# A fixed order for every engine through the opening stage of a fused attention and mixture kernel

## The chip, the core and the metric

The kernel runs on one core of a Trainium2 chip. The metric is the device time of one execution in microseconds. Three executions of the kernel before took 696.54, 697.15 and 697.70 us; the median is 697.15 us. The profile shown below is of the execution that took 697.70 us; its span, from the first to the last instruction, is 695.9 us.

Five engines work side by side, each on its own queue of instructions: TensorE (PE, with its weight loads as PEld), VectorE (DVE), ScalarE (ACT), GpSimd (POOL), and SyncE (SP), which here issues all transfers.

## What is computed

The reference has three stages, each fed by the one before. Chunked attention over 4 batches, 8 heads, 768 positions and head size 64:

```python
for c in range(nc):                       # chunks of 32 queries
    k_full = concat(mem_k, k[c*32-16 : c*32+40])
    v_full = concat(mem_v, v[c*32-16 : c*32+40])
    scores = scale * q_c @ k_full.T
    a = exp(scores - max(scores)); a = a / (sum(a) + 1e-9)
    out[c] = a @ v_full
```

Then a feed-forward layer over 3072 tokens, and a soft mixture of 8 experts:

```python
h = x @ w_in                              # 512 -> 2048
g = s * relu(h)**2 + b
y = g @ w_out                             # 2048 -> 512
logits = y @ phi                          # 32 slots
slot_input = softmax(logits, axis=0).T @ y
slot_out[e] = relu(slot_input[e] @ w1[e]) @ w2[e]
result = softmax(logits, axis=1) @ slot_out
```

## The kernel before, in words

The 3072 tokens are taken in six blocks of 512 (`NB`). A block has four **attention units** u, one for each pair of heads. The hidden layer has sixteen tiles of 128 (`NF`), so the feed-forward part is 96 steps n; step n takes hidden tile n mod 16 of block n div 16. A step issues 12 products into the hidden tile (`mm_h`), the activation (`make_g`), and, one step later, 12 products into the output (`mm_y`). Every operand is split into a high and a low part of a rounded format, so each product is three matmuls; ACT makes the high part and another engine subtracts it for the low part.

While PE works through block j, the attention of block j+1 and the mixture's statistics of block j-1 are slipped in between (`bg`). Only the four units of block 0 have nothing to hide behind: they run in an opening stage, before the first steps, and that stage is what the change rewrites.

The feed-forward weights come as 64-bit integers' worth of halves: 32 halves of 512 columns (two for each hidden tile: first the w_in half, then the w_out half), each loaded into a staging tile `sp`, decoded by four instructions and stored in `w`. The decode is one clamp on DVE, two passes on ACT, and a join on DVE (`w_decode`).

An attention unit goes through these instructions in turn: the query tile is spread into a block layout by ACT and DVE (`spread_q`); 16 small matmuls give the scores (`att_qk`, with a DVE memset or two on the scores' bank for the edges of the sequence); DVE takes the maximum and subtracts it, ACT takes the exponential, DVE sums, adds a constant and takes the reciprocal, and POOL multiplies (`att_soft`); PE transposes four blocks and two copies bring them to `pb` (`att_tr`); 16 small matmuls multiply with the values (`att_pv`), ACT writes the high part of x and DVE the low part.

The opening stage is written as a string of tokens, `START`, a letter and a number each. Letters: q, k, v and w are loads, c loads constants, z is a warming matmul on zeros, S spreads q, A is the score matmuls, F the softmax, T and t the transposes with their copies (T with both copies on ACT), P the value matmuls with both parts of x, D a decode, I and O the splits of the w_in and w_out half, H the first step's products with one of the four x tiles, y frees buffers.

Before the change, only PE and SP keep the order in which the code is written. For ACT, DVE and POOL a scheduler chooses the order, over the opening stage and the steps behind it together.

```python
    with tc.manual_schedule(engines={mybir.EngineType.PE, mybir.EngineType.SP}):
...
        for token in START.split():
            steps[token[0]](int(token[1:]))
```

Whatever is chosen, each engine then works through its list strictly in order, and an instruction that waits holds up everything behind it on that engine.

Of the kernel before, what the change touches and what calls it, by code (L numbers as in the profile page):

```python
# [11 lines left out]
AF = mybir.ActivationFunctionType  # L12
ALU = mybir.AluOpType
# [23 lines left out]
def tile_attention_moe_softmoe(  # L37
# [83 lines left out]
    def r32(ap):  # L121
        return ap.bitcast(F32R)
# [41 lines left out]
    def spread_q(u):  # L164
        t, src = qv(u), qsv(u)
        act.activation(out=t[0:64, :, 0, :], in_=src[0:64], func=AF.Copy)
        dve.tensor_copy(t[64:128, :, 1, :], src[64:128])

    def load_v(u):
        j, hp = divmod(u, NHP)  # L170
# [17 lines left out]
            if gc % 24 == 23:  # L188
                dve.memset(S[64 * par:64 * par + 64, t, 56:64], NEG)

    def att_soft(u, b, last=None):
        S = b.rearrange("p (t n) -> p t n", t=8)
        E = epv(u)
        mx, sm = ast[u % 2][:, 0, :], ast[u % 2][:, 1, :]
        dve.tensor_reduce(out=mx, in_=S, axis=AX.X, op=ALU.max)  # L195
        dve.tensor_tensor(out=E, in0=S, in1=mx.unsqueeze(2).to_broadcast([P, 8, 64]), op=ALU.subtract)  # L196
        act.activation(out=E, in_=E, func=AF.Exp, scale=0.125)  # L197
        dve.tensor_reduce(out=sm, in_=E, axis=AX.X, op=ALU.add)  # L198
        dve.tensor_scalar(out=sm, in0=sm, scalar1=EPS, scalar2=None, op0=ALU.add)  # L199
# [16 lines left out]
    def att_pv(u, b):  # L216
        j, hp = divmod(u, NHP)
        vt, pb = vv(u), pbv(u)
        for m in range(8):
            for h in range(2):  # L220
                pe.matmul(b[64 * h:64 * h + 64, 64 * m:64 * m + 64], lhsT=vt[:, m, h, :],  # L221
                          rhs=pb[:, m // 2, m % 2, h].rearrange("p z n -> p (z n)"), start=True, stop=True)
        xt = hl(X[j % 2][hp])
        act.activation(out=r32(xt[:, 0]), in_=b, func=AF.Copy)  # L224
        dve.tensor_tensor(out=r32(xt[:, 1]), in0=b, in1=xt[:, 0], op=ALU.subtract)  # L225


# [11 lines left out]
            sp.dma_start(out=t.bitcast(U32), in_=wd[f][:, 512 * h:512 * h + 512].bitcast(U32))  # L239
            stage_full.append((f, h, t))  # L240

    def w_decode():
        f, h, t = stage_full.pop(0)
        u = t.bitcast(U32).rearrange("p (n w) -> p n w", w=2)
        low, high = u[:, :, 0], u[:, :, 1]
        hv = t.rearrange("p (n w) -> p n w", w=2)[:, :, 1]
        top = t.bitcast(U8).rearrange("p (n b) -> p n b", b=8)[:, :, 3]
        dst = W[f][:, 512 * h:512 * h + 512].bitcast(U32)
        dve.tensor_scalar(out=hv, in0=hv, scalar1=-EXP_TOP, scalar2=EXP_TOP, op0=ALU.max, op1=ALU.min)
        act.activation(out=hv, in_=hv, func=AF.Prelu, scale=EXP_SHIFT, alpha=SIGN_SHIFT)  # L250
        act.activation(out=low, in_=top, func=AF.Copy, scale=1.0 / 32.0, bias=-31.0 / 64.0)
        dve.scalar_tensor_tensor(out=dst, in0=high, scalar=3, in1=low, op0=ALU.logical_shift_left,
                                 op1=ALU.bitwise_or)
        stage_free.append(t)


    def split_wi(n):
        t, raw = hl(WI[n % 2]), W[n % NF][:, 0:512]
        act.activation(out=r32(t[:, 0]), in_=raw, func=AF.Copy)  # L259
        (dve if n < NF else pool).tensor_tensor(out=r32(t[:, 1]), in0=raw, in1=t[:, 0], op=ALU.subtract)  # L260

    def split_wo(n):
        t, raw = hl(WO[n % 2]), W[n % NF][:, 512:1024]
# [197 lines left out]
    def run_bg(task):  # L461
        k, a = task
        if k == "qk":
            b = mbank()
            att_qk(a, b)
            if a + 2 < NB * NHP:
                load_q(a + 2)
                load_k(a + 2)
            att_soft(a, b)
        elif k == "tr":  # L470
            att_tr(a, mbank())
        elif k == "pv":
            att_pv(a, mbank())
            if a + 2 < NB * NHP:
                load_v(a + 2)
        elif k == "log":
            y_logits(a, mbank())
        elif k == "ytr":
            y_tr(a, mbank(), "act" if a % 2 else "dve")
        elif k == "etr":  # L480
            b = mbank()
            pe.transpose(b[:, 128:256], lts, ident)
            e_tr(b)
            dve.tensor_copy(lall[:, 4 * a:4 * a + 4, :], b[:, 128:256].rearrange("p (t s) -> p t s", t=4))
        elif k == "csoft":
            c_soft(a)
        elif k == "slot":
            slots(a, mbank())

    with tc.manual_schedule(engines={mybir.EngineType.PE, mybir.EngineType.SP}):  # L490
# [26 lines left out]
        def s_qk(u):  # L517
            sbk[u] = sbank()
            att_qk(u, sbk[u])


        steps = {
            "c": lambda _: sp.dma_start(out=cons, in_=cd),
# [3 lines left out]
            "S": spread_q,  # L527
            "w": w_load,
            "z": keep_warm,
            "t": lambda u: att_tr(u, sbank()),  # L530
            "A": s_qk,
            "F": lambda u: att_soft(u, sbk[u], pool),
            "T": lambda u: att_tr(u, sbank(), True),
            "P": lambda u: att_pv(u, sbank()),
            "D": lambda _: w_decode(),
            "I": split_wi,
            "O": split_wo,
# [279 lines left out]
```

## Time and profile before

| | us |
|---|---|
| median of 3 executions | 697.15 (696.54 to 697.70) |
| profiled execution | 697.70 |
| its span, first to last instruction | 695.9 |
| PE busy | 675.7 (97% of the span) |
| DVE busy | 357.7 (51%) |
| ACT busy | 353.6 (51%) |
| POOL busy | 216.7 (31%) |
| TensorE's mean granted clock | 0.99 of full |

PE is busy nearly throughout, so its gaps decide; they are few and lie at the two ends. A busy PE is not PE at its peak, since the ends of matmuls are modelled. The other engines are half busy on average, but that average hides one stretch, from 35 to 110 us, where DVE is nearly full.

### The profile page before, as it was taken

To read this page: it belongs to the slowest core of one execution; us is meant where nothing else is said; L and a number is where in the kernel's file an instruction comes from. 1 tells how busy PE (TensorE), PEld (TensorE's weight loads), DVE (VectorE), ACT (ScalarE), POOL (GpSimd) and SP (SyncE) were. 2 spreads that over 40 slices of the span, in tenths; PEclk is the share of its full clock that TensorE was granted. 3 is DMA by queue.
4 is the path that set the end of the run, shared out by engine and by line. 5 is a ranking of instruction groups with operands and counts; after the bars stand their busy time and mean duration, and the time that the engine had idled before them with its cause. 6 is when DMAs were issued, how large, how long until landed. Compare 5 with 4: busy or idle time off the path is not lost.

```text
span 695.9 us, 12228 instructions
## 1 busy us (share of the span) xinstructions
PE 675.7 (97%) x4953; PEld 533.3 (77%) x4953; DVE 357.7 (51%) x644; ACT 353.6 (51%) x628; POOL 216.7 (31%) x178
## 2 busy tenths in 40 slices
PE   7599999999999999999999999999999999999995
PEld 4488888888788888788888788888788888787353
DVE  5689997446534456544445444554553332223233
ACT  4779894544444445444445444545444544444332
POOL 4100000343344334334434334434334444441000
PEclk9799999999999999999999999999999999999998
DMA  9998802702201211211120221120123523628998
GB/s 348 389 336 328 270 40 91 284 32 80 91 16 77 91 42 50 91 52 64 68 75 18 91 67 56 61 91 1 62 84 129 211 92 91 211 92 272 237 294 348
DMA packets 47032, 94.38 MB, mean 136 GB/s; under 512 B 2944, under 2 KB 27520, under 8 KB 46976
## 3 DMA queue, kind: packets, MB, share of 16 engines
q1 hardware_dynamic: 46976, 93.60, 39.3%
q8 instruction: 39, 0.64, 0.4%
q14 instruction: 17, 0.14, 0.1%
HBM read 87.30 MB, written 6.29 MB: 134 GB/s over the span
## 4 chain that ended last, share of the span: by engine, by line
PE 95%; DVE 2%; ACT 1%; POOL 1%; issue 0%; POOLq 0%; DVEq 0%; ACTq 0%
PE bank L292 39%; PE bank L272 38%; PE bank L221 4%; PE bank L181 3%; PE bank L686 2%; PE bank L643 2%; PE bank L207 2%; PE bank L336 1%; PE bank L712 1%; PE bank L314 1%; PE bank L352 1%; PE bank L504 1%; PE bank L390 0%; POOL rt L201 0%; PE bank L662 0%
## 5 line engine op out<-in xcount | busy, mean ns | idle before, releaser
L292 PE MATMUL bank<-g,wo 128*128 128x512 f32 x1152 | 285.2, 396 | 0.0
L272 PE MATMUL bank<-x,wi 128*128 128x512 f32 x1152 | 278.6, 391 | 0.0
L272 PEld LDWEIGHTS bank<-x,wi 128*128 128x128 f32 x1152 | 217.1, 189 | 45.2
L292 PEld LDWEIGHTS bank<-g,wo 128*128 128x128 f32 x1152 | 211.1, 188 | 48.9 <-ACT wi L259 4.2
L279 DVE SCALAR_TENSOR_TENSOR rt<-bank,cons,rt 128x512 f32<-128x512 f32 x96 | 72.0, 750 | 228.3 <-ACT rt L278 228.1
L265 POOL TENSOR_TENSOR wo<-w,wo 128x512 fp32r<-128x512 f32 x80 | 103.2, 1290 | 204.9 <-ACT wo L264 200.9
L260 POOL TENSOR_TENSOR wi<-w,wi 128x512 fp32r<-128x512 f32 x80 | 103.4, 1293 | 188.8 <-ACT wi L259 188.8
L259 ACT ACTIVATE wi<-w 128x512 fp32r<-128x512 f32 x96 | 60.5, 630 | 148.3 <-PE bank L272 144.8
L280 ACT ACTIVATE g<-rt,cons 128x512 fp32r<-128x512 f32 x96 | 69.4, 723 | 42.6 <-DVE rt L279 41.3
L264 ACT ACTIVATE wo<-w 128x512 fp32r<-128x512 f32 x96 | 60.3, 628 | 55.2 <-PE bank L292 53.5
L281 DVE SCALAR_TENSOR_TENSOR g<-rt,cons,g 128x512 fp32r<-128x512 f32 x96 | 72.0, 750 | 27.3 <-ACT g L280 24.5
L278 ACT ACTIVATE rt<-bank 128x512 f32<-128x512 f32 x96 | 55.8, 581 | 5.4 <-PE bank L272 5.2
L197 ACT ACTIVATE ep<-ep 128x512 f32<-128x512 f32 x22 | 13.8, 627 | 30.1 <-DVE ep L196 30.1
L221 PEld LDWEIGHTS bank<-pb,v 128*64 128x64 f32 x704 | 22.3, 138 | 7.1 <-issue 6.7
L181 PEld LDWEIGHTS bank<-k,q 128*64 128x64 f32 x704 | 22.4, 138 | 5.6 <-issue 4.5
L181 PE MATMUL bank<-k,q 128*64 128x64 f32 x704 | 24.7, 223 | 1.7 <-ACT ep L197 1.7
L221 PE MATMUL bank<-pb,v 128*64 128x64 f32 x704 | 25.3, 225 | 0.0
L198 DVE TENSOR_REDUCE ast<-ep 128x8 f32<-128x512 f32 x22 | 15.1, 685 | 9.8 <-ACT ep L197 9.7
L225 DVE TENSOR_TENSOR x<-bank,x 128x512 fp32r<-128x512 f32 x24 | 16.5, 688 | 0.6 <-ACT x L224 0.5
L224 ACT ACTIVATE x<-bank 128x512 fp32r<-128x512 f32 x24 | 14.3, 596 | 4.9 <-PE bank L221 2.5
L195 DVE TENSOR_REDUCE ast<-bank 128x8 f32<-128x512 f32 x24 | 16.4, 683 | 0.4
L199 DVE TENSOR_SCALAR ast<-ast 128x8 f32<-128x8 f32 x24 | 15.9, 664 | 0.7
(237 smaller groups left out, 522.6 us busy)
## 6 DMA issues: line engine op xcount, KB each, us to landing
k<-kd SPq DMA_DIRECT2D x22, 512.0 KB, 6.1
sp<-wd SPq DMA_DIRECT2D x22, 512.0 KB, 8.8
v<-vd SPq DMA_DIRECT2D x22, 512.0 KB, 3.9
q<-qd SPq DMA_DIRECT2D x20, 512.0 KB, 5.3
w<-e1d SPq DMA_DIRECT2D x10, 512.0 KB, 3.4
out<-w SPq DMA_DIRECT2D x9, 512.0 KB, 6.2
sp<-e1d SPq DMA_DIRECT2D x7, 512.0 KB, 7.9
sp<-e2d SPq DMA_DIRECT2D x7, 512.0 KB, 7.2
```

Of the source, the lines that this page charges most:

```text
L181: pe.matmul(S[64 * par:64 * par + 64, 2 * i + z, :], lhsT=qt[:, c].rearrange("p h n -> p (h n)"), rhs=kt[:, c, :], start=True, stop=True)
L221: pe.matmul(b[64 * h:64 * h + 64, 64 * m:64 * m + 64], lhsT=vt[:, m, h, :], rhs=pb[:, m // 2, m % 2, h].rearrange("p z n -> p (z n)"), sta ...
L259: act.activation(out=r32(t[:, 0]), in_=raw, func=AF.Copy)
L260: (dve if n < NF else pool).tensor_tensor(out=r32(t[:, 1]), in0=raw, in1=t[:, 0], op=ALU.subtract)
L264: act.activation(out=r32(t[:, 0]), in_=raw, func=AF.Copy)
L265: (dve if n < NF else pool).tensor_tensor(out=r32(t[:, 1]), in0=raw, in1=t[:, 0], op=ALU.subtract)
L272: pe.matmul(HB[n % 2], lhsT=r32(w[:, a, kt, :]), rhs=r32(x[:, b]), start=(kt == 0 and i == 0), stop=(kt == 3 and i == 2))
L278: act.activation(out=r, in_=HB[n % 2], func=AF.Relu, scale=1.0 / WSCALE ** 2)
L279: dve.scalar_tensor_tensor(out=t, in0=HB[n % 2], scalar=s_col, in1=r, op0=ALU.mult, op1=ALU.mult)
L280: act.activation(out=r32(g[:, 0]), in_=t, func=AF.Identity, bias=b_col)
L281: dve.scalar_tensor_tensor(out=r32(g[:, 1]), in0=t, scalar=b_col, in1=g[:, 0], op0=ALU.add, op1=ALU.subtract)
L292: pe.matmul(YB[dt], lhsT=r32(w[:, a, dt * 128:dt * 128 + 128]), rhs=r32(g[:, b]), start=(f == 0 and i == 0), stop=(f == NF - 1 and i == 2))
```

## The change

The string is rewritten and its steps are cut finer. The softmax is split into m (maximum, subtraction, exponential) and n (sum, reciprocal, multiplication on POOL); the value matmuls P no longer include the low part of x, which is x; a decode is D (clamp and the two ACT passes) and E (the join); the split of a w_in half is I and i. The DVE half of spreading q moves to POOL for every unit but the first. T3 gets one of its two copies on DVE, and T0 both on ACT. One warming matmul is added ahead of A0, and two instead of one stand between A0 and A1. The loads of the second and third staged halves come later in the list of transfers. And the whole string is put under a fixed order for ACT, DVE and POOL too.

```diff
 START = (
-    "q0 k0 w1 c0 q1 k1 q2 k2 v0 w1 q3 k3 v1 w1 v2 v3 w1 "
-    "z3 S0 A0 F0 z1 S1 D0 A1 z1 S2 t0 z1 A2 P0 F1 S3 T1 F2 "
-    "I0 A3 k4 w1 q4 w1 k5 P1 v4 w1 T2 q5 H0 P2 F3 T3 P3 y0 H1 w9 H2 D0 v5 D0 D0"
+    "q0 k0 w1 c0 q1 k1 q2 k2 v0 q3 k3 v1 w1 v2 w1 v3 w1 "
+    "z4 S0 A0 z1 D0 m0 S1 z1 A1 E0 n0 S2 I0 m1 A2 T0 i0 n1 m2 z1 S3 P0 T1 A3 x0 n2 m3 D1 P1 x1 T2 E1 n3 H0 D2 P2 x2 E2 "
+    "k4 w1 q4 w1 k5 v4 w1 q5 H1 T3 P3 H2 x3 D3 E3 y0 w9 v5"
 )
...
         act.activation(out=t[0:64, :, 0, :], in_=src[0:64], func=AF.Copy)
-        dve.tensor_copy(t[64:128, :, 1, :], src[64:128])
+        (pool if u else dve).tensor_copy(t[64:128, :, 1, :], src[64:128])
...
-    def att_soft(u, b, last=None):
+    def att_exp(u, b):
         S = b.rearrange("p (t n) -> p t n", t=8)
-        E = epv(u)
-        mx, sm = ast[u % 2][:, 0, :], ast[u % 2][:, 1, :]
+        E, mx = epv(u), ast[u % 2][:, 0, :]
...
+    def att_norm(u, last=None):
+        E, sm = epv(u), ast[u % 2][:, 1, :]
...
+    def att_low(u, b):
+        j, hp = divmod(u, NHP)
+        xt = hl(X[j % 2][hp])
         dve.tensor_tensor(out=r32(xt[:, 1]), in0=b, in1=xt[:, 0], op=ALU.subtract)
...
+    def w_end():
+        f, h, t = half_done.pop(0)
+        low, high, hv, top, dst = w_views(f, h, t)
         dve.scalar_tensor_tensor(out=dst, in0=high, scalar=3, in1=low, op0=ALU.logical_shift_left,
                                  op1=ALU.bitwise_or)
...
-        for token in START.split():
-            steps[token[0]](int(token[1:]))
+        with tc.manual_schedule(engines={mybir.EngineType.Activation, mybir.EngineType.DVE, mybir.EngineType.Pool}):
+            for token in START.split():
+                steps[token[0]](int(token[1:]))
```

What this does to the lists of the engines is seen in three places. First, ACT's list at its beginning. `q0` and `q1` are the spread queries of units 0 and 1, `sp0` the first staged half, `ep` the exponentials, `w14` holds the raw queries of units 2 and 3. Before:

```order
L166 ACTIVATE q0_97<-rt1_96 64x16x32
L251 ACTIVATE sp0_110<-sp0_110 128x512
L250 ACTIVATE sp0_110<-sp0_110 128x512
L166 ACTIVATE q1_98<-rt1_96 64x16x32
L259 ACTIVATE wi0_81<-w0_65 128x512
L197 ACTIVATE ep_109<-ep_109 128x512
L166 ACTIVATE q0_97<-w14_79 64x16x32
```

The same place in the changed kernel:

```order
L166 ACTIVATE q0_97<-rt1_96 64x16x32
L262 ACTIVATE sp0_110<-sp0_110 128x512
L263 ACTIVATE sp0_110<-sp0_110 128x512
L196 ACTIVATE ep_109<-ep_109 128x512
L166 ACTIVATE q1_98<-rt1_96 64x16x32
L166 ACTIVATE q0_97<-w14_79 64x16x32
L280 ACTIVATE wi0_81<-w0_65 128x512
```

The spread of q1 has moved behind the exponential of unit 0 (L196, L197 before), and the order of the decode's two passes is swapped.

Second, DVE's list at its beginning. `bank1` and `bank2` hold the scores of units 0 and 1, `ast0` and `ast1` their maxima and sums. Before:

```order
L167 COPY q0_97<-rt1_96 64x16x32
L249 TENSOR_SCALAR sp0_110<-sp0_110 128x512
L187 MEMSET bank1_140 64x16
L195 TENSOR_REDUCE ast0_135<-bank1_140 128x8
L252 SCALAR_TENSOR_TENSOR w0_65<-sp0_110 128x512
L196 TENSOR_TENSOR ep_109<-bank1_140,ast0_135 128x512
L167 COPY q1_98<-rt1_96 64x16x32
L260 TENSOR_TENSOR wi0_81<-w0_65,wi0_81 128x512
L198 TENSOR_REDUCE ast0_135<-ep_109 128x8
L167 COPY q0_97<-w14_79 64x16x32
L199 TENSOR_SCALAR ast0_135<-ast0_135 128x8
L187 MEMSET bank2_141 64x16
```

The same place in the changed kernel:

```order
L167 COPY q0_97<-rt1_96 64x16x32
L187 MEMSET bank1_140 64x16
L261 TENSOR_SCALAR sp0_110<-sp0_110 128x512
L194 TENSOR_REDUCE ast0_135<-bank1_140 128x8
L195 TENSOR_TENSOR ep_109<-bank1_140,ast0_135 128x512
L187 MEMSET bank2_141 64x16
L269 SCALAR_TENSOR_TENSOR w0_65<-sp0_110 128x512
L200 TENSOR_REDUCE ast0_135<-ep_109 128x8
L201 TENSOR_SCALAR ast0_135<-ast0_135 128x8
L202 RECIPROCAL ast0_135<-ast0_135 128x8
L194 TENSOR_REDUCE ast1_136<-bank2_141 128x8
L195 TENSOR_TENSOR ep_109<-bank2_141,ast1_136 128x512
```

The memset on each unit's scores, which waits for that unit's score matmuls, now stands ahead of the clamp of sp0 (for unit 0) and ahead of the join of w0 and of unit 0's sum (for unit 1).

Third, DVE's list from unit 3's maximum (the reduce on `bank1`) to its reciprocal (on `ast1`); `x01` and `x02` are the x tiles of units 1 and 2, `rt0` holds the exponentials of units 2 and 3. Before:

```order
L195 TENSOR_REDUCE ast1_136<-bank1_140 128x8
L265 TENSOR_TENSOR wo0_83<-w0_65,wo0_83 128x512
L225 TENSOR_TENSOR x01_86<-bank2_141,x01_86 128x512
L196 TENSOR_TENSOR rt0_95<-bank1_140,ast1_136 128x512
L249 TENSOR_SCALAR sp2_112<-sp2_112 128x512
L198 TENSOR_REDUCE ast1_136<-rt0_95 128x8
L252 SCALAR_TENSOR_TENSOR w1_66<-sp2_112 128x512
L225 TENSOR_TENSOR x02_87<-bank6_145,x02_87 128x512
L199 TENSOR_SCALAR ast1_136<-ast1_136 128x8
L260 TENSOR_TENSOR wi1_82<-w1_66,wi1_82 128x512
L200 RECIPROCAL ast1_136<-ast1_136 128x8
```

The same place in the changed kernel:

```order
L194 TENSOR_REDUCE ast1_136<-bank1_140 128x8
L195 TENSOR_TENSOR rt0_95<-bank1_140,ast1_136 128x512
L261 TENSOR_SCALAR sp1_111<-sp1_111 128x512
L261 TENSOR_SCALAR sp4_114<-sp4_114 128x512
L231 TENSOR_TENSOR x01_86<-bank2_141,x01_86 128x512
L269 SCALAR_TENSOR_TENSOR w0_65<-sp1_111 128x512
L200 TENSOR_REDUCE ast1_136<-rt0_95 128x8
L201 TENSOR_SCALAR ast1_136<-ast1_136 128x8
L293 TENSOR_TENSOR wo0_83<-w0_65,wo0_83 128x512
L202 RECIPROCAL ast1_136<-ast1_136 128x8
```

The low part of x01 and the split of wo0 (L293) now stand between unit 3's subtraction and its reciprocal, and so does work of later steps, which the scheduler has put between the fixed instructions: the clamp of `sp4` is not in the string. ACT's list has the same in that place: between the two copies of T2 and those of T3 stand, in this order, a pass of sp4, the high part of wo0, the other pass of sp4, one of sp5, two of sp2 and the high part of x02.

## Rows read from the trace of the kernel before

**Rows 1.** The page: PE's busy share in 40 equal slices of the span.

```profile
PE   7599999999999999999999999999999999999995
```

**Rows 2.** Busy us (instructions) of PE, PEld, DVE, ACT, POOL by stretch; clock, DMA share, GB/s.

```profile
0.00:35.00 35.00, 23.17 (x288) 15.40 (x289) 21.93 (x47) 20.39 (x34) 9.17 (x17) 0.88 0.94 367
35.00:110.00 75.00, 75.00 (x521) 61.68 (x521) 71.22 (x138) 62.92 (x112) 0.00 (x0) 0.99 0.69 245
110.00:600.00 490.00, 490.00 (x3272) 399.21 (x3271) 234.54 (x400) 234.95 (x413) 193.33 (x150) 1.00 0.23 79
```

**Rows 3.** PE's waits up to 42 us: total us, times, longest.

```profile
PE bank L207 <- POOL rt L201: 5.8, 2, 3.4
```

**Rows 4.** Timeline of PE: start us, us, what, [idle before <-releaser].

```profile
1.31 5.08 PE L504 MATMUL bank<-w 128*128 128x512 f32 x6 [1.31 <-POOL w L500]
6.32 1.15 PE L181 MATMUL bank<-k,q 128*64 128x64 f32 x32
7.40 1.12 PE L504 MATMUL bank<-w 128*128 128x512 f32 x2
10.26 1.15 PE L181 MATMUL bank<-k,q 128*64 128x64 f32 x32 [1.74 <-ACT ep L197]
...
13.49 0.66 PE L207 MATMUL bank<-cons,ep 128*128 128x128 f32 x4 [1.02 <-POOL ep L201]
...
14.94 1.15 PE L181 MATMUL bank<-y,q 128*64 128x64 f32 x32
...
18.23 1.15 PE L181 MATMUL bank<-y,q 128*64 128x64 f32 x32 [0.28 <-ACT q L166]
...
22.88 1.11 PE L207 MATMUL bank<-cons,rt 128*128 128x128 f32 x4 [2.40 <-POOL rt L201]
...
25.34 1.59 PE L221 MATMUL bank<-pb,yt 128*64 128x64 f32 x32
30.32 1.12 PE L207 MATMUL bank<-cons,rt 128*128 128x128 f32 x4 [3.40 <-POOL rt L201]
32.80 1.97 PE L221 MATMUL bank<-pb,yt 128*64 128x64 f32 x32 [1.36 <-ACT pb L212]
34.70 5.91 PE L272 MATMUL bank<-x,wi 128*128 128x512 f32 x21
...
41.62 3.02 PE L292 MATMUL bank<-g,wo 128*128 128x512 f32 x12
```

**Rows 5.** Timeline of POOL, ACT and DVE: one of each kind of instruction.

```profile
3.47 0.52 POOL L512 MEMSET pb<- 64x512 f32 x1
6.89 0.67 ACT L250 ACTIVATE sp<-sp 128x512 f32<-128x512 f32 x1
8.27 0.68 DVE L252 SCALAR_TENSOR_TENSOR w<-sp 128x512 uint32<-128x512 uint32 x1
9.59 0.63 ACT L197 ACTIVATE ep<-ep 128x512 f32<-128x512 f32 x1
10.65 0.68 DVE L198 TENSOR_REDUCE ast<-ep 128x8 f32<-128x512 f32 x1
11.36 0.42 DVE L167 COPY q<-w 64x512 f32<-64x512 f32 x1
12.02 0.20 DVE L200 RECIPROCAL ast<-ast 128x8 f32<-128x8 f32 x1
12.40 1.04 POOL L201 TENSOR_TENSOR ep<-ep,ast 128x512 f32<-128x512 f32 x1 [6.54 <-DVE ast L200]
35.45 0.69 DVE L225 TENSOR_TENSOR x<-bank,x 128x512 fp32r<-128x512 f32 x1 [0.20 <-ACT x L224]
```

**Rows 6.** PE by stretch: busy us (instructions), granted clock, DMA share, GB/s.

```profile
20.00:23.00 3.00, 0.60 (x19) 0.99 1.03 419
23.00:26.00 3.00, 2.94 (x19) 0.50 1.02 415
30.00:36.00 6.00, 4.32 (x39) 0.50 0.76 294
```

More of the change, by code (lines that the diff above doesn't have):

```diff
@@ L240, in w_load, with w_views @@
             stage_full.append((f, h, t))
-    def w_decode():
-        f, h, t = stage_full.pop(0)
+    def w_views(f, h, t):
         u = t.bitcast(U32).rearrange("p (n w) -> p n w", w=2)
@@ L248, in w_decode, with w_begin @@
         dst = W[f][:, 512 * h:512 * h + 512].bitcast(U32)
+        return low, high, hv, top, dst
+    half_done = []
+    def w_begin():
+        f, h, t = stage_full.pop(0)
+        low, high, hv, top, dst = w_views(f, h, t)
         dve.tensor_scalar(out=hv, in0=hv, scalar1=-EXP_TOP, scalar2=EXP_TOP, op0=ALU.max, op1=ALU.min)
@@ L251, in w_decode @@
         act.activation(out=low, in_=top, func=AF.Copy, scale=1.0 / 32.0, bias=-31.0 / 64.0)
+        half_done.append((f, h, t))
+    def w_end():
+        f, h, t = half_done.pop(0)
+        low, high, hv, top, dst = w_views(f, h, t)
         dve.scalar_tensor_tensor(out=dst, in0=high, scalar=3, in1=low, op0=ALU.logical_shift_left,
@@ L254, in w_decode, with wi_high, wi_low, split_wi @@
         stage_free.append(t)
-    def split_wi(n):
+    def w_decode():
+        w_begin()
+        w_end()
+    def wi_high(n):
         t, raw = hl(WI[n % 2]), W[n % NF][:, 0:512]
         act.activation(out=r32(t[:, 0]), in_=raw, func=AF.Copy)
+    def wi_low(n):
+        t, raw = hl(WI[n % 2]), W[n % NF][:, 0:512]
         (dve if n < NF else pool).tensor_tensor(out=r32(t[:, 1]), in0=raw, in1=t[:, 0], op=ALU.subtract)
+    def split_wi(n):
+        wi_high(n)
+        wi_low(n)
     def split_wo(n):
@@ L468, in run_bg @@
                 load_k(a + 2)
-            att_soft(a, b)
+            att_exp(a, b)
+            att_norm(a)
         elif k == "tr":
@@ L472, in run_bg @@
         elif k == "pv":
-            att_pv(a, mbank())
+            b = mbank()
+            att_pv(a, b)
+            att_low(a, b)
             if a + 2 < NB * NHP:
@@ L519, in s_qk, with s_pv @@
             att_qk(u, sbk[u])
+        def s_pv(u):
+            sbk[u] = sbank()
+            att_pv(u, sbk[u])
         steps = {
@@ L529, in tile_attention_moe_softmoe @@
             "z": keep_warm,
-            "t": lambda u: att_tr(u, sbank()),
             "A": s_qk,
[L532 to L537, printed above, removed]
+            "m": lambda u: att_exp(u, sbk[u]),
+            "n": lambda u: att_norm(u, pool),
+            "T": lambda u: att_tr(u, sbank(), u < 3),
+            "P": s_pv,
+            "x": lambda u: att_low(u, sbk[u]),
+            "D": lambda _: w_begin(),
+            "E": lambda _: w_end(),
+            "I": wi_high,
+            "i": wi_low,
             "H": lambda kt: mm_h(0, (kt,)),
```

## The prediction

> **What bounds the kernel now.** I began with the page's slices: PE stands at nine tenths or more from the third slice on, and only the first two and the last show room [rows 1]. The busy times by stretch make that exact. From 35 to 110 us PE is busy 75.00 of 75.00 us, from 110 to 600 us 490.00 of 490.00, but only 23.17 of 35 us in the opening stage [rows 2]. So from 35 us PE sets the pace and has no gap in which lost time could be won back, and whatever moves the start of the first output products (L292 in the timeline, 41.62 us, [rows 4]) moves the end by the same amount. I call that start Y0; the forecast is how far it moves.
>
> In the opening stage nothing is full: DVE is busy 21.93 of 35 us and ACT 20.39 [rows 2]. It is a chain. The waits of PE say which: 5.8 us for POOL's multiplication in units 2 and 3, the longest 3.4 us [rows 3], that is the end of a softmax that crosses PE, DVE, ACT, DVE and POOL. The timeline gives the steps: A0 at 6.32, A1 10.26, T0 13.49, A2 14.94, A3 18.23, T2 22.88, P2 25.34, T3 30.32, P3 32.80, then 21 feed-forward matmuls from 34.70 to 40.6, and Y0 [rows 4].
>
> **The change part by part.** Almost nothing is added or removed: one warming matmul, three copies moved from DVE to POOL. What changes is what stands ahead of what on each engine, so I walked the new lists from A0 to Y0, each instruction starting when its engine and its inputs are ready, with the durations of the timeline: sum, join, subtraction and low part 0.69 on DVE, reciprocal 0.20 and the constant before it 0.17, decode pass 0.67 and exponential 0.63 on ACT, multiplication 1.04 on POOL [rows 5], score matmuls 1.15 [rows 4]. The same walk over the old lists puts T3 at 30.3 and Y0 at 41.6, where the trace has 30.32 and 41.62, so the method is worth about half a us.
>
> The one operation without a row is POOL's copy of 64x512. Below it stands POOL's memset of the same shape, 0.52; above it a copy with twice the data and a second input would be the multiplication, 1.04; DVE does the copy in 0.42 [rows 5]. With a margin I use 0.5 to 1.2 as ends and 0.85 as value, between the two POOL rows. The Trainium skill (GPSIMD Engine Reference, Engine selection) says that a one-input operation runs on GpSimd at about the rate of VectorE, which no run here shows yet; by it each copy would cost about 0.42 and, with two copies on the chain, my sum would come out 0.9 us smaller.
>
> *A0.* The first three warming matmuls take 5.08 us, 0.85 for each of six records; the later ones take 1.12 for two records [rows 4]. The fourth costs about 1.0 at that rate. A0 moves from 6.32 to 7.4: **+1.1**.
>
> *A1.* The score matmuls end at 8.55. DVE's list now has the memset on them first, so the clamp of sp0, which ran while A0 was still running, comes after: memset 0.07, clamp 0.42, maximum 0.69, subtraction 0.69, to 10.5. ACT follows with the exponential to 11.15, and only then with its half of q1's spread, which now stands behind it: 11.75. A1 starts at 11.8 instead of 10.26: **+1.5**. The old list had this spread done early; A1 did not depend on unit 0's softmax.
>
> *A2 and T0.* A1 ends at 12.95. The memset on unit 1's scores now stands ahead of the join of w0 and of unit 0's sum, so a softmax whose exponential was ready at 11.15 waits for A1. Then 0.07, 0.69, 0.69, 0.17, 0.20 and small gaps: reciprocal at 14.9, POOL's multiplication to 16.0. POOL's list is in order too: its copy for q2 stands behind it, to 16.9. A2 waits for that: 16.9 instead of 14.94, **+2.0**. T0, ready at 16.0, stands behind A2 in PE's list: 17.9 at full clock, against 13.49.
>
> Here the clock enters. In the old run PE idled 2.4 us ahead of T2, and the stretch from 23 to 26 us shows 0.50 granted, the lower of the two levels; the same again from 30 to 36 us, after the idle 3.4 us [rows 4, 6]. Between A1 and A2 PE will now idle about 4 us, longer than either. So I take A2 and T0 at the lower level, as T2 and P3 were (1.11 and 1.97 instead of 0.66 and 1.15, [rows 4]): T0 at 18.9, **+5.4** (+4.4 at full clock).
>
> *A3 and T2.* The same pattern twice more. The memset on unit 2's scores holds wi0's low part and unit 1's sum; then multiplication, copy for q3, and ACT's half of the spread behind unit 2's exponential: A3 at 23.8 instead of 18.23, **+5.6** (+4.5). The memset on unit 3's scores holds x00's low part and unit 2's sum: reciprocal at 26.9, T2 at 28.0 instead of 22.88, **+5.1** (+4.0).
>
> *P2 and T3.* ACT now has unit 3's exponential, two passes of sp1 and the high part of x01 ahead of T2's copies: from 28.3, 0.63 + 2 x 0.67 + 0.60 + 2 x 0.59, so P2 starts at 31.9 instead of 25.34. Behind the copies stand a pass of sp4 and the high part of wo0, to 33.1; DVE's reciprocal for unit 3 stands behind wo0's low part: 33.8, then 34.0, POOL to 35.1. T3 at 35.1 instead of 30.32, **+4.8** (+3.7).
>
> *P3 to Y0.* ACT has two passes of sp2 and x02 ahead of T3's first copy, DVE the low part of x02 and a join ahead of the second: P3 at 38.1 instead of 32.80. At the lower clock it ends at 40.1; high and low part of x03 are there at 41.7, against 36.14 in the old run [rows 5]: **+5.5**. H1 has been done by then, which gives back some tenths. Fifteen matmuls and the score matmuls of unit 4 take PE to 46.5. On ACT, the high part for step 2, two passes of sp3, the activation, a pass of sp0 and wo1's high part stand ahead of the first g: 46.9. Y0 at about 46.6 instead of 41.62: **+5.0**.
>
> *Costed at nothing.* The three copies taken from DVE (3 x 0.42) give nothing, since DVE is waiting where they stood. The later loads of sp1 and sp2 cost nothing, since their decodes start at 28 us, long after; the same holds for the transfers behind them on SP's queue that now wait for sp2 and sp3 to be joined, as they bring weights of step 4 and later, 20 us ahead of use. If that cover were gone PE would stall in the steps (third rival). From Y0 on the lists hold the same work, and at Y0 one staged half more has been joined than before.
>
> The profiled execution took 697.7; with +5.0 it is 702.7. The median of the runs shown lies 0.55 below that execution, so I forecast **702.2**. Full clock throughout and a copy of 0.5 give +3.2 (then the first g, behind ACT's list, is what Y0 waits for); a copy of 1.2 and the lower clock up to Y0 give +6.5.
>
> **The rivals.** *Faster: the idle time fills.* DVE idles 13 and ACT 15 of the first 35 us [rows 2]; three units in flight could fill this, remove the waits of 5.8 us before T2 and T3 [rows 3], and, less the 1.1 for the warming matmul and about as much for the clock, give -3.5: 693.7. The Trainium skill speaks for it (Perfetto Trace Analysis, Optimization Strategy): interleaving regimes with different limits may improve performance. What decides is whether T3 starts before 30.3. Against it, T3 depends on A3's softmax, A3 on POOL's copy behind unit 1's multiplication, and that on A2: in the list the units are chained to each other more than before. Chance 0.08.
>
> *No change.* If POOL's copies cost little and the memsets rarely held DVE, A2 and A3 would keep their old times, T3 would start within 1.4 us of 30.3, and the end would stay within 0.2% (1.4 us, about what this kernel's measurement can tell from nothing): 697.2. Against it, the first +1.5 at A1 rests only on rows of PE, DVE and ACT that are known. Chance 0.06.
>
> *Slower by more: PE starves in the decode stretch.* DVE is busy 71.22 of 75 us from 35 to 110 us [rows 2]. If its order there is worse, or halves arrive late because SP waits for sp3's join (about 45 us), PE would wait before some of the first 14 steps, for a few tenths to a us each: 3 to 6 us more, about 706.5. It decides if any weight split ends after PE has finished the step before. Against it, DVE starts the stretch one half ahead. Chance 0.12.
>
> **How the numbers follow.** My own case has 0.74, at 702.2, with 700.4 to 703.7 as its bounds. To leave out no more than 2 in 10 the range takes in half of the slower rival's span, up to 705.5, and reaches down to 699.0 for a walk that errs by more than its test showed; the faster case and no change stay out (0.14). Faster 0.08, same 0.06, slower 0.86.
>
> **What the profile after would show.** A1 near 11.8, A2 near 16.9 with its wait put down to POOL's copy of q, T0 behind A2, T3 near 35, Y0 near 46.6, and PE busy without a gap from there, each later step shifted alike. I am wrong if A2 starts by 15.5, if T3 starts before 31, or if PE's steps after Y0 are closer or wider apart than before. The copy on POOL should take 0.5 to 1.2; the granted clock should be at its lower level at A2 or T0.

## The result and the profile after

The changed kernel takes **702.76 us** (median; 701.87 to 703.67), the kernel before 697.42 (696.54 to 698.53): a ratio of 1.0076 with an interval of 1.0056 to 1.0096, slower by 5.3 us. The profiled execution took 703.02, its span is 701.2.

First the timeline of PE in the changed kernel, start and duration in us, with the idle time ahead and what ended it:

```profile
1.31 6.14 PE L535 MATMUL bank<-w 128*128 128x512 f32 x8 [1.31 <-POOL w L531]
7.38 1.15 PE L181 MATMUL bank<-k,q 128*64 128x64 f32 x32
...
11.75 1.15 PE L181 MATMUL bank<-k,q 128*64 128x64 f32 x32 [1.31 <-ACT q L166]
16.62 1.98 PE L181 MATMUL bank<-y,q 128*64 128x64 f32 x32 [3.72 <-ACT ep L196]
18.53 1.12 PE L209 MATMUL bank<-cons,ep 128*128 128x128 f32 x4
...
22.95 1.15 PE L181 MATMUL bank<-y,q 128*64 128x64 f32 x32 [0.27 <-issue]
...
27.13 0.66 PE L209 MATMUL bank<-cons,rt 128*128 128x128 f32 x4 [1.37 <-POOL rt L203]
...
30.67 1.98 PE L223 MATMUL bank<-pb,yt 128*64 128x64 f32 x32 [2.19 <-ACT pb L214]
...
34.02 1.05 PE L209 MATMUL bank<-cons,rt 128*128 128x128 f32 x4
37.00 1.97 PE L223 MATMUL bank<-pb,yt 128*64 128x64 f32 x32 [1.92 <-DVE pb L216]
38.90 5.05 PE L300 MATMUL bank<-x,wi 128*128 128x512 f32 x18
43.88 1.15 PE L181 MATMUL bank<-k,q 128*64 128x64 f32 x32
44.99 3.01 PE L320 MATMUL bank<-g,wo 128*128 128x512 f32 x12
...
57.58 0.66 PE L209 MATMUL bank<-cons,ep 128*128 128x128 f32 x4 [1.41 <-DVE ep L203]
...
59.24 3.03 PE L320 MATMUL bank<-g,wo 128*128 128x512 f32 x12
```

The rows are to be laid beside [rows 4]. A0 is 1.06 later, A1 1.49, A2 1.68, T0 5.04, A3 4.72, T2 4.25, P2 5.33, T3 3.70, P3 4.20 and Y0 (44.99) 3.37. The second thing to see is the row at 57.58: PE, dense from Y0 on in the kernel before, waits 1.41 us ahead of unit 4's transposes, between the output products of steps 1 and 2. I call the start of step 2's output products Y2. It goes from 54.25 to 59.24, 4.99 later, and every later step I looked at lies 5.0 later (128.24 and 133.25, 551.31 and 556.32). So the opening costs 3.4, of which 1.06 is there at A0, behind the fourth warming matmul, and 2.31 arises from A0 to Y0. This wait and what goes with it cost 1.6. The last 0.3 is idle time of PE at the far end (8.6 us behind 600 us, 8.3 before).

The stretches of the changed kernel, PE, PEld, DVE, ACT and POOL busy, clock, DMA share, GB/s:

```profile
0.00:35.00 35.00, 24.08 (x260) 15.90 (x260) 16.63 (x39) 17.65 (x29) 11.07 (x20) 0.88 0.94 365
35.00:110.00 75.00, 71.67 (x529) 58.86 (x529) 70.44 (x135) 63.58 (x114) 0.00 (x0) 0.96 0.62 227
110.00:600.00 490.00, 490.00 (x3272) 399.18 (x3271) 238.05 (x407) 235.18 (x413) 191.44 (x148) 1.00 0.23 81
...
16.00:20.00 4.00, 3.38 (x37) 3.04 (x38) 1.30 (x4) 0.94 (x2) 0.57 (x1) 0.57 1.03 410
20.00:24.00 4.00, 3.49 (x70) 2.48 (x68) 1.59 (x4) 3.12 (x7) 1.65 (x2) 1.00 1.03 409
30.00:40.00 10.00, 7.41 (x74) 6.08 (x75) 8.47 (x16) 8.05 (x14) 1.05 (x1) 0.51 0.64 251
40.00:44.00 4.00, 4.00 (x21) 3.01 (x21) 3.49 (x7) 3.16 (x7) 0.00 (x0) 0.95 0.00 0
```

Beside [rows 2] DVE does 5.3 us less work in the first 35 us and ACT 2.7 less: 1.3 of DVE's are the copies now on POOL; for the rest the fixed lists leave both idle, and the work comes after. From 35 to 110 us PE lacks 3.33 us, the wait of 1.92 ahead of P3 and that of 1.41 in step 2. In the last row the DMA engines move nothing for 4 us.

How a fixed list loses time is best seen on DVE at unit 0's softmax, start, duration and idle time:

```profile
9.78 0.69 DVE L195 TENSOR_TENSOR ep<-bank,ast 128x512 f32<-128x512 f32 x1
12.96 0.67 DVE L269 SCALAR_TENSOR_TENSOR w<-sp 128x512 uint32<-128x512 uint32 x1 [2.49 <-ACT q L166]
12.98 0.07 DVE L187 MEMSET bank<- 64x16 f32 x1
13.55 0.68 DVE L200 TENSOR_REDUCE ast<-ep 128x8 f32<-128x512 f32 x1
...
14.47 0.20 DVE L202 RECIPROCAL ast<-ast 128x8 f32<-128x8 f32 x1
```

and on POOL behind it:

```profile
14.85 1.04 POOL L203 TENSOR_TENSOR ep<-ep,ast 128x512 f32<-128x512 f32 x1 [4.78 <-DVE ast L202]
15.96 0.61 POOL L167 COPY q<-w 64x512 f32<-64x512 f32 x1
```

Unit 0's exponential has ended at 11.13. Its sum (L200) starts at 13.55, behind the memset on unit 1's scores, which A1 makes (11.75 to 12.90), while DVE is idle for 2.49 us. The profile names ACT's spread (L166) for this wait, but both spreads have ended by 12.2; what ends last ahead of it is A1. POOL's multiplication waits for the reciprocal, the copy for q2 behind it, and A2 for that copy, which ends at 16.57. The profile puts A2's wait down to unit 1's exponential, which ends at 16.62 but feeds nothing of A2; in e3 below, where the two again end within 0.1 of each other, it names POOL's copy.

The wait in step 2 is found in two views. SP's longest wait from 34 to 70 us, by total, times, longest:

```profile
SPq L245 <- DVE w L269: 15.8, 5, 6.8
```

and the chain of work that ended last, from 43.96 on (start, us, what):

```profile
43.96 0.37 SPq L245
...
44.43 7.30 DMA yt<-wd
...
51.74 0.02 ACT yt L263
51.77 0.54 issue
52.31 0.59 ACT rt L306
...
56.92 0.61 DVE ep L203
...
57.58 0.66 PE bank L209 x4
```

SP stands 6.8 us at a transfer that needs a staging tile back from a join; the transfers into `yt` and `y` stand behind it, though their tiles are free by 39 (P3, which reads yt last, ends at 38.97). They go out at 43.95, after the 4 us in which nothing moved. ACT's list has the decode passes on yt ahead of step 2's activation (L306), so ACT waits until 51.74, then DVE's list runs late, down to the multiplication that unit 4's transposes need.

### The profile page after: what moved, and what is told of

Its sections match the earlier page's. It is cut to its first block, busy times and chain, and to the rows that moved or that the text cites. A ratio compares the mean times of both kernels' runs of the same rounds, so it can differ in the third digit from the quotient of the medians.

```text
span 701.2 us, 12236 instructions
## 1 busy us (share of the span) xinstructions
PE 678.3 (97%) x4955; PEld 535.1 (76%) x4955; DVE 355.8 (51%) x641; ACT 353.5 (50%) x628; POOL 219.0 (31%) x181
## 4 chain that ended last, share of the span: by engine, by line
PE 92%; DMA 3%; DVE 2%; ACT 1%; issue 1%; POOL 0%; SPq 0%; ACTq 0%; POOLq 0%
PE bank L320 38%; PE bank L300 36%; PE bank L223 4%; PE bank L181 3%; PE bank L681 2%; PE bank L724 2%; PE bank L209 1%; PE bank L364 1%; DMA v<-vd 1%; DMA yt<-wd 1%; PE bank L342 1%; PE bank L535 1%; PE bank L380 1%; PE bank L750 1%; DMA out<-w 1%
## 5 line engine op out<-in xcount | busy, mean ns | idle before, releaser
L293 POOL TENSOR_TENSOR wo<-w,wo 128x512 fp32r<-128x512 f32 x80 | 103.3, 1292 | 205.3 <-ACT wo L292 205.3
L306 ACT ACTIVATE rt<-bank 128x512 f32<-128x512 f32 x96 | 55.7, 581 | 4.6 <-PE bank L300 4.6
L196 ACT ACTIVATE ep<-ep 128x512 f32<-128x512 f32 x22 | 13.8, 627 | 28.4 <-DVE ep L195 28.2
L200 DVE TENSOR_REDUCE ast<-ep 128x8 f32<-128x512 f32 x22 | 15.1, 685 | 9.1 <-ACT ep L196 9.0
L262 ACT ACTIVATE sp<-sp 128x512 f32<-128x512 f32 x24 | 15.9, 671 | 7.5 <-DVE sp L261 7.4
L269 DVE SCALAR_TENSOR_TENSOR w<-sp 128x512 uint32<-128x512 uint32 x24 | 17.0, 718 | 3.5 <-ACT q L166 2.5
```

The lines of the kernel that those rows point to most:

```text
L306: act.activation(out=r, in_=HB[n % 2], func=AF.Relu, scale=1.0 / WSCALE ** 2)
```

## The experiments

All times are medians, ratios are to the kernel before on the same chip, whose median there was 697.81, 697.86 or 698.28. A0 itself lies anywhere from 5.6 to 8.0 in the profiled executions, by how many warming matmuls there are and how long they take, so I compare the way from A0 to Y0. The starts are from PE's timelines (us), each of one profiled execution, which can lie off its kernel's median (e9: 693.86 beside 695.44; e3: 702.37 beside 701.13):

| kernel | A0 | T0 to P0 | T3 | Y0 | A0 to Y0 | Y0 to Y2 | time |
|---|---|---|---|---|---|---|---|
| before | 6.32 | 2.43 | 30.32 | 41.62 | 35.30 | 12.63 | 697.4 |
| changed | 7.38 | 2.41 | 34.02 | 44.99 | 37.61 | 14.25 | 702.8 |
| e1 order not fixed | 7.66 | 4.64 | 31.03 | 41.85 | 34.19 | 12.63 | 698.1 |
| e2 copies on DVE | 7.62 | 2.52 | 32.20 | 44.27 | 36.65 | 12.87 | 700.2 |
| e3 q1 first | 7.98 | 2.76 | 33.41 | 45.23 | 37.25 | 13.87 | 701.1 |
| e4 loads as before | 7.09 | 2.41 | 33.73 | 44.60 | 37.51 | 12.81 | 701.4 |
| e5 units first | 7.30 | 2.41 | 30.58 | 44.63 | 37.33 | 13.25 | 703.1 |
| e6 before, fixed | 6.53 | 3.31 | 40.47 | 59.02 | 52.49 | 12.64 | 715.0 |
| e7 fixed, reordered | 7.56 | 1.95 | 28.54 | 45.05 | 37.49 | 12.63 | 700.1 |
| e8 free, three edits | 6.37 | 2.42 | 26.97 | 37.73 | 31.36 | 12.82 | 693.5 |
| e9 free, copies on DVE | 6.75 | 2.50 | 26.87 | 37.33 | 30.58 | 12.63 | 695.4 |
| e10 free, three warming | 5.64 | 5.56 | 30.79 | 42.10 | 36.46 | 12.63 | 698.2 |
| e11 free, loads as before | 6.82 | 5.63 | 31.17 | 41.68 | 34.86 | 12.62 | 698.0 |

My theory was that the fixed order is the loss, because ready work stands behind waiting work; the rivals were that the new list, the copies on POOL or the fourth warming matmul are. The fourth warming matmul is taken out alone only with the order free (e10), not with the order fixed.

**The new list without the fixed order** (e1).

```diff
-        with tc.manual_schedule(engines={mybir.EngineType.Activation, mybir.EngineType.DVE, mybir.EngineType.Pool}):
-            for token in START.split():
-                steps[token[0]](int(token[1:]))
+        for token in START.split():
+            steps[token[0]](int(token[1:]))
```

> The changed kernel with the fixed order of ACT, DVE and POOL taken away; the new string, the finer steps, POOL's copies and the order of the transfers stay. Theory (the loss is in what stands ahead of what on the three engines): Y0, the start of the first output products, falls from 44.99 to between 38 and 41.6 us, and the time to between 695 and 698.5, at or below the kernel before. Rival (the loss is in the string itself: the extra warming matmul, the copies on POOL, the later loads): Y0 stays above 43.5 and the time above 701.

698.09 us, ratio 1.000 (0.999 to 1.0011). The whole loss is gone, the wait in step 2 too. Y0 at 41.85 is just past the late end of the range: PE waits in a new place, at P0.

```profile
16.06 0.66 PE L209 MATMUL bank<-cons,ep 128*128 128x128 f32 x4 [1.70 <-POOL ep L203]
...
20.70 1.98 PE L223 MATMUL bank<-pb,v 128*64 128x64 f32 x32 [3.12 <-ACT pb L214]
```

ACT in the same kernel:

```profile
18.86 0.69 ACT L263 ACTIVATE sp<-sp 128x512 uint32<-128x512 uint8 x1 [1.43 <-DMA sp<-wd]
19.45 0.57 ACT L212 ACTIVATE pb<-bank 64x512 f32<-64x512 f32 x1
20.05 0.59 ACT L214 ACTIVATE pb<-bank 64x512 f32<-64x512 f32 x1
```

T0's copies (L212, L214) stand behind a decode pass on a half that lands at 18.8. A free order has its own such mistakes; this one comes back below.

**The kernel before with a fixed order** (e6), the other half of this test: on the lists as its own string writes them.

```diff
-        for token in START.split():
-            steps[token[0]](int(token[1:]))
+        with tc.manual_schedule(engines={mybir.EngineType.Activation, mybir.EngineType.DVE, mybir.EngineType.Pool}):
+            for token in START.split():
+                steps[token[0]](int(token[1:]))
```

> The kernel before with one edit: ACT, DVE and POOL keep the order in which its own opening list is written, as the changed kernel does with its list. Theory: the fixed order is itself the cost, since as written the pieces of a softmax stand ahead of ready work of other units; the order that the scheduler finds for the kernel before is much better than its list. Walking the fixed lists with the durations of before, T3 starts at about 37 instead of 30.3 and Y0 at 50 to 56 instead of 41.6, so the time is 706 to 712. Rival: what costs is the new list (pieces, copies on POOL), not fixing as such. Then this kernel stays within 1 us of 697.4.

714.97 us, ratio 1.0245 (1.0228 to 1.0262): the theory's side, and 3 us more than its range. PE's waits show where:

```profile
24.96 1.12 PE L207 MATMUL bank<-cons,ep 128*128 128x128 f32 x4 [5.93 <-POOL ep L201]
...
40.47 1.11 PE L207 MATMUL bank<-cons,rt 128*128 128x128 f32 x4 [6.60 <-POOL rt L201]
```

So fixing alone costs some 17 us, the new list alone nothing, both together 5.3. The new list wins back most of what fixing takes away, but not all; which of its parts does so (finer pieces, their order, the copies) no run takes apart.

**The three copies back on DVE, order fixed** (e2).

```diff
-        (pool if u else dve).tensor_copy(t[64:128, :, 1, :], src[64:128])
+        dve.tensor_copy(t[64:128, :, 1, :], src[64:128])
```

> The changed kernel with the DVE half of every spread of q back on DVE; all else stays, the fixed order too. Theory (A2 and A3 start late since POOL's copy stands behind a multiplication): the copies for units 2 and 3 no longer wait for a softmax, A2 comes some 2 us earlier, Y0 near 42 and the time near 699.5 to 700.5. Rival (A2 and A3 wait for the softmax by other ways, PE's and DVE's lists): Y0 stays within 0.7 of 44.99 and the time within 1 of 702.8.

700.24 us, ratio 1.0029 (1.0015 to 1.0044). The time is as expected, the way there is not: A0 to Y0 is only 0.96 shorter, and Y0 to Y2 1.38, since PE has no wait in step 2 left. In that run yt's transfer goes out 1.63 ahead of Y0 instead of 1.04, and ACT no longer waits for it.

**q1's spread ahead of unit 0's softmax** (e3).

```diff
-    "z4 S0 A0 z1 D0 m0 S1 z1 A1 ...
+    "z4 S0 A0 z1 S1 D0 m0 z1 A1 ...
```

> The changed kernel with one token moved: the spread of q1 (S1) stands ahead of the decode and of unit 0's maximum, subtraction and exponential. Theory (ACT's half of it waits for the exponential, and with A1 everything behind it): A1 starts near 10.3 instead of 11.75, Y0 near 42.5 to 43.5, the time near 700.5. Rival (the chain is held elsewhere, so an earlier A1 only lengthens the waits): A1 moves, Y0 stays within 0.5 of 44.99 and the time within 1 of 702.8.

701.13 us, ratio 1.0044 (1.0028 to 1.0059). A1 comes 1.38 earlier behind A0, Y0 only 0.36: for Y0 the rival was right, and the time lies between the two. A2 then waits 3.7 us for POOL's copy of q. One place mended, the chain waits at the next.

**The late loads in the order of before** (e4): the tiles yt and y are put second in the list of free staging tiles instead of last.

```diff
-            "y": lambda _: stage_free.extend(YT + Y),
+            "y": lambda _: stage_free.__setitem__(slice(1, 1), YT + Y),
```

> The changed kernel with the list of late loads in the order of before: behind the eighth staged half come the yt and y buffers, and the buffers sp1 to sp3, which wait for their joins, come last. Theory (SP waits for sp3's join until 43.95, the transfers pause, ACT then waits for yt until 51.7 and PE 1.4 us in step 2): Y0 stays at 45, the 1.4 us ahead of the transposes of unit 4 go to under 0.4, and the time is near 701.3. Rival (that wait comes from DVE's list, not from the transfers): the 1.4 us and 702.8 stay.

701.4 us, ratio 1.0049 (1.0031 to 1.0067). A0 to Y0 is unchanged (37.51 beside 37.61), Y0 to Y2 takes 12.81 instead of 14.25, and the row of 1.41 is gone: 1.44 us, as the theory had it. This rests on the trace; the time fits it (701.4 beside 702.76), but its interval overlaps that of the change. In place of the empty 4 us the same stretches now read:

```profile
40.00:42.00 2.00, 2.00 (x10) 1.59 (x9) 2.00 (x5) 1.36 (x3) 0.00 (x0) 1.00 0.97 324
42.00:44.00 2.00, 2.00 (x23) 1.45 (x24) 1.58 (x3) 2.00 (x5) 0.00 (x0) 1.00 0.95 246
```

**Units 2 and 3 ahead of the decodes, order fixed** (e5). Beside e1 the changed kernel is 1.0 us later at T2, 3.0 at T3 and 3.2 at P3, so it loses 2.2 us between T2 and P3 (the 3.0 below is the lag at T3). I took this stretch for the place.

```diff
-    "... A3 x0 n2 m3 D1 P1 x1 T2 E1 n3 H0 D2 P2 x2 E2 "
-    "k4 w1 q4 w1 k5 v4 w1 q5 H1 T3 P3 H2 x3 D3 E3 y0 w9 v5"
+    "... A3 x0 n2 m3 P1 T2 n3 x1 H0 P2 D1 T3 x2 E1 P3 x3 "
+    "k4 w1 q4 w1 k5 v4 w1 q5 H1 H2 D2 E2 D3 E3 y0 w9 v5"
```

> The changed kernel with its fixed list rewritten behind unit 3's exponential: the tokens of unit 2's and 3's transposes and products (P1 T2 n3 x1 H0 P2 T3 x2 P3 x3) go ahead of the decode passes of sp1, sp2 and sp3 (D1 E1, D2 E2, D3 E3), so that neither two passes of sp1 nor x01 stand ahead of T2's copies and only one decode stands between T2 and T3's copies. Against the kernel with the free order, the changed kernel loses 3.0 us between T2 and P3 and 3.1 at Y0. Theory: these last links of the attention chain are what sets Y0. Then T3 starts at about 31 instead of 34.0, P3 at about 34 instead of 37.0, Y0 at about 42 instead of 45.0, and the time is 699.8 (699 to 700.6). Rival: Y0 is set as much by the decodes that feed steps 0 to 2, which this edit puts 1 to 3 us later on ACT and DVE. Then T3 and P3 come early all the same, but PE waits for the parts of wi1 at step 1, Y0 moves by under 1 us, and the time is 702 to 703.

703.11 us, ratio 1.0078 (1.006 to 1.0096): the rival, and that theory falls. T3 comes 3.44 earlier and P3 (33.73) 3.27, as expected, and Y0 just 0.36. PE now waits in the first step's products instead:

```profile
33.73 1.98 PE L223 MATMUL bank<-pb,yt 128*64 128x64 f32 x32 [2.50 <-DVE pb L216]
35.63 2.88 PE L300 MATMUL bank<-x,wi 128*128 128x512 f32 x9
40.30 3.32 PE L300 MATMUL bank<-x,wi 128*128 128x512 f32 x12 [1.78 <-ACT wi L280]
```

and ACT shows why:

```profile
35.75 0.60 ACT L226 ACTIVATE x<-bank 128x512 fp32r<-128x512 f32 x1 [1.71 <-PE bank L223]
36.24 0.62 ACT L292 ACTIVATE wo<-w 128x512 fp32r<-128x512 f32 x1
37.44 0.68 ACT L262 ACTIVATE sp<-sp 128x512 f32<-128x512 f32 x1 [0.57 <-DVE sp L261]
```

Now the decode of the next w_in half is what stands behind: ACT idles 1.71 us for P3 while the passes of sp2 are in the list behind x03. Two chains, attention and decode, share ACT and DVE and end nearly together; a fixed list can put one ahead of the other, and then the other sets Y0. This is read from the lists; no run holds one chain and frees the other.

**All places mended at once, order fixed** (e7): e5 with S1, S2 and S3 ahead of the softmax steps that they stood behind, and e4's loads.

```diff
-    "z4 S0 A0 z1 D0 m0 S1 z1 A1 E0 n0 S2 I0 m1 A2 T0 i0 n1 m2 z1 S3 P0 T1 A3 ...
+    "z4 S0 A0 z1 S1 D0 m0 z1 A1 E0 S2 n0 I0 m1 A2 T0 i0 S3 n1 m2 z1 P0 T1 A3 ...
```

> The changed kernel, its order still fixed, with the three places mended that the traces name: the halves of q1, q2 and q3's spread ahead of the exponential and the sums that they stood behind (S1 ahead of D0 m0, S2 ahead of n0, S3 ahead of n1), units 2 and 3 ahead of the decodes as in the run with the units first, and the late loads in the order of before. Theory: the fixed order costs only at these places. From A0 to Y0 it takes about 33.3 us instead of 37.6, the 1.4 us wait in step 2 is gone, and the time is 697 (696 to 698.5), as before the change. Rival: as with q1's copy alone, the chain is held elsewhere: A2 and T0 come earlier, Y0 by 1 us or less, and with the wait gone the time is 700 to 701.

700.13 us (697.3 to 702.0), ratio 1.0033 (1.0018 to 1.0047): nearer the rival. T3 starts at 28.54, 5.5 us earlier than in the change, and Y0 at 45.05. The same wait for wi is there, and the clock goes against it:

```profile
33.20 4.21 PE L300 MATMUL bank<-x,wi 128*128 128x512 f32 x9
39.19 4.71 PE L300 MATMUL bank<-x,wi 128*128 128x512 f32 x12 [1.78 <-ACT wi L280]
```

The 12 products behind the wait take 4.71 us where e5 has 3.32; the granted clock is 0.59 in 40:44 here and 1.00 there. The executions of this kernel lie far apart, and the profiled one, at 701.24, is 1.1 above their median, so part of its Y0 is this clock. What mending the places is worth at full clock stays open, and so does why A0 to Y0 (37.49) is no shorter than in the change (37.61).

**The order free, with three edits** (e8): e1 with three warming matmuls, q's copies on DVE, and the loads of before.

```diff
-    "z4 S0 A0 ...
+    "z3 S0 A0 ...
...
-        (pool if u else dve).tensor_copy(t[64:128, :, 1, :], src[64:128])
+        dve.tensor_copy(t[64:128, :, 1, :], src[64:128])
...
-            "y": lambda _: stage_free.extend(YT + Y),
+            "y": lambda _: stage_free.__setitem__(slice(1, 1), YT + Y),
```

> The changed kernel with the order free again, three warming matmuls ahead of unit 0 instead of four, all of q's copies on DVE, and the late loads in the order of before. With the free order alone the time was 698.1, Y0 41.85, and PE waited 3.1 us for T0's copies behind passes of sp1, whose transfer came late. Theory: the pieces are worth something once the rest is undone: A0 about 0.9 earlier, POOL's copies off the path, Y0 between 36 and 39.5, and the time 692.5 to 696, faster than both kernels. Rival: the wait for sp1's decode passes keeps its place and A0's gain is lost in it: Y0 41 or later, 697 to 698.

693.47 us, ratio 0.9937 (0.9923 to 0.9951): 4.4 us faster than before and some 9 faster than the change. A0 to Y0 takes 31.36. The next three runs take the edits apart, each alone with the free order: e9 has the second piece of this diff, e10 the first, e11 the third.

> The changed kernel with the order free, and q's three copies back on DVE; four warming matmuls and the late loads as in the change. It takes apart the 4.6 us that the kernel with three warming matmuls, the copies on DVE and the loads of before gained on the one with the free order alone (698.1 to 693.5). Theory: most of it is the copies. On POOL they stand in one list with the multiplications that the units wait for, and with them gone unit 0's copies no longer stand behind passes of sp1: T0 is followed by P0 within 3 us instead of 4.6, Y0 lies 31 to 32.5 us behind A0 instead of 34.2, and the time is 695.7 (694.8 to 696.6). Rival: it is the warming matmul, which lets the other engines' work fall better; then the time here stays at 697.5 to 698.5.

695.44 us, ratio 0.9966 (0.9951 to 0.9982): the theory. A0 to Y0 falls from 34.19 to 30.58, a little below its range, the time by 2.6.

> The changed kernel with the order free and three warming matmuls ahead of unit 0 instead of four; copies on POOL and loads as in the change. Theory: A0 comes 0.9 to 1.2 earlier, but part of it is lost where T0's copies stand behind passes of sp1, whose transfer comes at a fixed time: 697.5 (696.8 to 698.2), against 698.1 with four. Rival: the whole chain moves with A0, 697.0, or more than this if the clock falls better.

698.16 us, ratio 0.9995 (0.9982 to 1.0007): no gain at all. A0 is 2.0 earlier than in e1 and Y0 not earlier; P0 lies 5.56 behind T0.

> The changed kernel with the order free and the late loads in the order of before; copies and warming matmuls as in the change. With the free order alone PE had no wait in step 2, although the loads stood in the changed order. Theory: nothing, 698.1 (697.4 to 698.8): the order of the late loads costs time only where a join that SP waits for comes late. Rival: part of the 4.6 us between the two free kernels is the loads, 696 to 697.

697.98 us, ratio 1.0002 (0.9988 to 1.0015): nothing, as expected.

Why the copies decide can be read in ACT's list. In e1, and in e10 and e11 alike, the scheduler has put a pass of sp1 ahead of T0's copies:

```
L196 ACTIVATE rt0_95<-rt0_95 128x512
L263 ACTIVATE sp1_111<-sp1_111 128x512
L212 ACTIVATE pb0_103<-bank6_145 64x16x32
L214 ACTIVATE pb0_103<-bank6_145 64x16x32
```

In e8 and e9 the pass stands behind them and behind unit 1's too. ACT in e8:

```profile
14.45 0.63 ACT L196 ACTIVATE ep<-ep 128x512 f32<-128x512 f32 x1 [2.52 <-DVE ep L195]
15.86 0.59 ACT L212 ACTIVATE pb<-bank 64x512 f32<-64x512 f32 x1 [0.77 <-PE bank L209]
16.47 0.59 ACT L214 ACTIVATE pb<-bank 64x512 f32<-64x512 f32 x1
...
20.33 0.69 ACT L263 ACTIVATE sp<-sp 128x512 uint32<-128x512 uint8 x1
```

So the copies seem to be worth 2.6 here not by their own 0.61 us each but because the scheduler chooses another list. In e11, with the copies on POOL, T0 starts at 14.62, ahead of e9's 14.91, and P0 yet 2.84 later. No run holds the copies and changes that place alone, so this is argued, and why the scheduler chooses so is not seen. Nor is it why the other two edits, worth nothing alone, come to about 2 us beside the copies (0.9937 against 0.9966): the profiled executions of e8 and e9, 693.61 and 693.86, hardly differ, so no trace shows these 2 us.

## Why the prediction was right, and where its steps were off

The time came out at 702.76 where 702.2 was forecast, and at 703.02 for the profiled execution where the sum said 702.7. The reason was right: e1 shows that the loss is the fixed order. That it comes about by work that stands behind waiting work is read from the lists and the timelines; single edits show it for A1 (e3) and for the transfers into yt (e4). But the sum has two errors that cancel, so that the time came within 0.6 is luck. The start of the steps moved by 3.4 and not 5.0, near the forecast's lower end of 3.2, and one of the costs put at nothing is 1.4 to 1.6.

**The links of the sum.** From A0 on, forecast and measured:

| | A0 | A1 | A2 | T0 | A3 | T2 | P2 | T3 | P3 | Y0 |
|---|---|---|---|---|---|---|---|---|---|---|
| forecast | 7.4 | 11.8 | 16.9 | 18.9 | 23.8 | 28.0 | 31.9 | 35.1 | 38.1 | 46.6 |
| measured | 7.38 | 11.75 | 16.62 | 18.53 | 22.95 | 27.13 | 30.67 | 34.02 | 37.00 | 44.99 |

The walk's reasons held at each link: A1 behind q1's spread, unit 0's sum behind the memset on unit 1's scores, A2 with POOL's copy, T0 behind A2. The 1.6 are four terms of the sum that were mis-sized. Up to A2 0.3, nearly all POOL's copy, taken at 0.85 and measured at 0.61. From T0 to A3 0.5: another copy, and the clock, which was at its lower level at A2 and T0 as forecast (0.57 from 16 to 20 us, 1.98 and 1.12 us in the timeline) but back at full level from 20 on (1.00). From T2 to T3 0.2. And from P3 to Y0 0.5: the forecast let PE stand until x03's low part, but 18 matmuls were left, and they run from 38.90 without a gap. Two places of the sum do not fit in themselves: P2's terms add up to 32.05 and not 31.9, and the first g stands at 46.9, behind the Y0 of 46.6 that needs it. Both lie within the half us that the walk claims.

The copy of 0.61 lies between the bounds, nearer the memset of the same shape (0.52) than the multiplication. The Trainium skill (GPSIMD Engine Reference, Engine selection) puts a one-input operation at about VectorE's rate; the trace has 0.61 against 0.42 on DVE [rows 5], so half as much again. The measurement decides: the sum by 0.61 would have been 0.5 smaller, by 0.42 0.9.

**Costed at nothing.** The step that failed is "the same holds for the transfers behind them on SP's queue that now wait for sp2 and sp3 to be joined, as they bring weights of step 4 and later, 20 us ahead of use". The use that counted was not the matmul but the decode pass, which ACT's list has 6 to 8 us behind the transfer's issue and ahead of step 2's activation. e4 puts this at 1.44 us. The "slower by more" rival named this mechanism and this join, with 3 to 6 us; the place was right and the price too high. So PE is not busy without a gap from Y0 on, as the forecast said; from Y2 to 600 us it is. One of the forecast's own signs of being wrong, steps after Y0 wider apart than before, came true here.

**The copies off DVE** were put at nothing in themselves, and their two on POOL on the chain. Back on DVE with the order fixed they gain 0.96 up to Y0 (e2), somewhat less than the two links of 0.61 that go; the further 1.4 in step 2 the forecast did not have.

**The rivals.** "Faster" had the right idea of what three units in work can do: once the order is free and POOL's copies are gone, T3 starts at 26.97, before its mark of 30.3, and the time is 693.5 (e8), beside its 693.7. What kept it from happening in the change is what the prediction held against it, units that are chained to each other in the list. "No change" would have been so without the fixed order: 698.1 (e1).

**What I had wrong after the result.** That an earlier A1 brings Y0 to 42.5 to 43.5 (e3: 45.23), and the copies back on DVE to 42 (e2: 44.27); that the stretch from T2 to P3 sets Y0 (e5), and that mending the named places gives the time of before (e7). In the last two the decodes took over.

## What to carry to other kernels

A fixed order can cost wherever an instruction that must wait stands ahead of one that is ready, though mending one such place may only show the next: write the engine's list down, mark the first instruction that waits for another engine, and read what is queued behind it. Where two chains share the same engines and end together, moving one ahead can gain next to nothing at the end, however much it moves its own steps (here 3.4 us at T3 and 0.36 at Y0). A transfer has slack only to the first instruction that touches its data in any engine's list, since all that stands behind that instruction waits with it.

## What the runs showed of the hardware

The warming matmuls at the very beginning take different times with the same list: three of them 5.08 us before the change, 5.13 in e8 and 4.40 in e10, four 6.14 in the change, 6.74 in e3 and 5.51 in e9. The granted clock shows 1.00 from 1.3 us up to A0 before the change and after it, so the rows do not say why. A0 lies over 1 us apart among the profiled executions whose opening list begins alike (6.75 in e9, 7.98 in e3), and starts are better compared from A0 on. And a matmul's duration here is a matter of the stretch, not of the code: the same 12 products took 3.32 us in e5 and 4.71 in e7, at a granted clock of 1.00 and 0.59, and in both PE had waited 1.78 us just before. In e7 it had stood at 0.50, the lower of the two levels, from 30 to 33 us already, in e5 at 1.00. From 38 to 40 us, though, both show 1.00; e7 then falls back to 0.50 from 41 to 44. What makes it fall in e7 alone is not shown.
